# Gate columns moved beside v, four small VectorE steps per batch folded away, and the order of all steps written out

## The chip, the cores and the metric

The kernel runs on one core of one Trainium2 chip. TensorE (PE) multiplies matrices, VectorE (DVE) and ScalarE (ACT) do elementwise work, GpSimd (POOL) does elementwise work and indirect DMAs, and the SyncE queue (SP) issues the other DMAs. The metric is the time of one execution in device microseconds (us), as the median of several runs.

## What is computed

Linear attention feeds a mixture of experts that sends each token to one expert. There are 8 batches, 8 heads, 576 positions and a head width of 64; the experts take 4608 tokens of width 512, there are 8 of them, and their hidden width is 1024.

```python
q_s = exp(q - max(q, -1)); q_s /= sum(q_s, -1) + 1e-9
k_s = exp(k - max(k, 2));  k_s /= sum(k_s, 2) + 1e-9
x = einsum('bhsd,bhde->bhse', q_s, einsum('bhsd,bhse->bhde', k_s, v))   # rows of 512
logits = x @ w_gate; expert = argmax(logits); p = softmax(logits)[expert]
out = p * (relu(x @ w1[expert]) @ w2[expert])
```

## The kernel before

The program has two parts. The **attention stage** goes through the 8 batches. A batch is cut into steps, each a short Python function named by two or three letters, the batch and a number. A planner (`Plan.emit`) with a table of costs (`COST`), a table of due times (`WHEN`) and a list of fills (`FILL`) decides in which order the steps are written out; every engine then works through its own list in that order. The **expert stage** is a loop over tiles of up to 384 tokens of one expert, with the two matrix products in split precision (three products each, lines 983 and 999).

The steps of a batch b, with the lines at which the profile shows them:

- `LK`, `LV`, `LQ` load k, v and q (lines 206 to 223; on SP). q has one buffer, so `LQ` of a batch waits until the one before has been used up.
- `KM0` to `KM4` find the maximum of k (lines 340 to 358): `KM0` takes maxima of two tensors in SBUF on DVE (`kp`, `km`), `KM2` and `KM4` transpose on PE.
- `KS`, `KE`, `KR`, `ER` subtract it (DVE, line 374) and take exponentials (ACT, line 378).
- `KV` multiplies k by v (PE, line 392). A column of ones beside v gives the sums over k; `N0` adds two of its parts, `N1` adds 1e-9 (line 402) and takes the reciprocal, `N2` scales into the tile `kx` (ACT, line 410).
- `G0` to `G3` form `kx` times `w_gate` and put the result, 16 columns, at the end of each of the four blocks of `kx`, behind 128 columns of v and 2 of ones.
- `QM` takes maxima of q (DVE, line 457), `QS` subtracts on POOL (line 462), `QE` does a quarter of the work on ACT (line 476), and `QMR` and `QSR` do the remaining rows of two batches together.
- Per 128 tokens, `TR` transposes (PE), `EX` takes the exponential (ACT), `MM` multiplies by `kx` (PE, lines 515 and 518), `DE` and `RE` make the reciprocal of the denominators (DVE), and `EV` writes the result with two multiplies (DVE): line 530 the gate columns into `lh`, line 532 the 512 values into a row of `xr`.
- Routing of a batch (`LS`, `R0` to `RH`, lines 562 to 624, nearly all on DVE) sums the gate columns over the heads, finds the expert, and counts ranks with a product on PE (`R5`). `PU` (POOL, line 628) sends each row of 520 floats to its expert's place in the table `xs` in DRAM.

`WG`, `WH`, `WL` bring in w1 of expert 0, eight parts through three buffers; `IL` reads the first 384 rows back when batches 0 to 4 are sent; `L1` (line 720) and `L4` (line 734) are the expert products of that first tile, written out inside the attention stage. Step tables (`T0` to `T9`) follow. **Fills** (line 194) are products of ones that are never read, placed ahead of named steps on PE.

Two of the steps that the text below speaks of most:

```python
def n1():
    TS(ks, ks, EPS, None, op0=ALU.add)
    nc.vector.reciprocal(o.kr, ks)
```

Of the kernel before, what the change touches and what calls it, by code (L numbers as in the profile page):

```python
# [24 lines left out]
WARM, WARM0, WARMD = 40, 4.0, 0.6  # L25
HOT = 384
ON_ACT = (1, 1, 1, 1, 1, 1, 1, 1)
COST = dict(VG=1.5, VH=1.0, VL=1.2, LK=3.3, LV=4.0, LQ=3.3, CD=1.1, CS=1.31, KM0=2.2, KM1=0.7, KM2=0.45, KM3=0.6, KM4=0.95,
            KR=0.6, ER=0.58, KS=0.6, KE=0.58, VC=1.411, VR=0.52, KV=0.85, N0=0.1, N1=0.25, N2=0.67, G0=0.5, G1=0.56, G2=1.0,
            G3=0.18, QM=2.2, QE=0.48, QMR=0.6, QS=1.9, QSR=1.1, TR=0.48, EX=0.545, MM=1.05, DE=0.12, RE=0.16, EV=0.75, LS=0.6,  # L30
            R0=0.15, R1=0.17, R3=0.12, R4=0.12, R5=0.1, R6=0.13, R7=0.1, R8=0.15, R9=0.17, RA=0.1, RB=0.1, RC=0.11, RD=0.1,
            RE_=0.1, RF=0.1, RG=0.1, RH=0.14, PU=1.13, WM=0.22, WG=0.75, WH=0.54, WL=1.3, IC=0.062, ID=0.07, IL=2.25, IT=0.43,
            IH=0.57, IX=0.64, IM=0.1, IN=0.13, L1=2.08, L2=0.49, L3=0.55, L4=5.6, T0=0.049, T1=0.4, T2=0.2, T3=0.041, T4=0.13, T5=2.6,
            T6=0.33, T7=0.25, T8=0.6, T9=0.6, PD=7.0, SW=0.0)
WHEN = dict(VG=112.97, VH=65.802, VL=234.696, WM=178.215, LK=-4.311, LV=-2.99, LQ=-2.988, CS=-160.111, CD=-2.432, KM0=186.18,
            KM1=182.9, KM2=-234.498, KM3=140.412, KM4=-65.994, KR=-100.451, ER=-11.026, KS=48.242, KE=-18.137, VC=128.428,
            VR=170.02, KV=-48.753, N0=161.745, N1=-131.023, N2=90.74, G0=-78.547, G1=-207.944, G2=2.387, G3=-189.242, QM=-84.744,
            QE=-340.111, QMR=-76.618, QS=-126.151, QSR=-25.154, TR=47.844, EX=-122.752, MM=67.147, DE=-122.56, RE=-49.933,
            EV=23.487, LS=80.974, R0=-147.601, R1=102.567, R3=-18.581, R4=-14.182, R5=38.348, R6=-9.574, R7=-183.452,
            R8=-116.162, R9=-214.4, RA=-219.99, RB=-108.906, RC=-268.039, RD=-23.486, RE_=-237.132, RF=29.438, RG=-216.006,  # L40
            RH=126.679, PU=95.896, WG=2.331, WH=-51.233, WL=-94.387, IC=109.395, ID=319.612, IL=0.595, IT=-86.61, IH=55.938,
            IX=158.381, IM=-20.084, IN=-124.88, L1=172.533, L2=98.456, L3=63.079, L4=63.079, T0=-143.724, T1=85.977, T2=96.711, T3=-20.217,
            T4=135.561, T5=67.264, T6=-338.231, T7=192.024, T8=-120.773, T9=1000.0, PD=179.626, SW=73.996)
WINDOW = 0.0
FILL = """
KM2.0.0.24 KM4.0.0.1 KM2.1.0.18 KM4.1.0.4 KV.0.0.1 KV.0.1.1 KM2.2.0.13 G2.0.0.1 KV.1.1.1 KV.1.2.1 KM2.3.0.4 G0.1.0.7
KM4.3.0.1 TR.1.2.1 KV.2.2.1 R5.0.0.2 MM.1.4.4 KV.3.2.1 G0.3.0.9 TR.3.2.1 G2.3.0.2 KV.4.0.1 KV.4.1.1 KV.4.2.1 KM2.5.0.16
KV.4.3.2 R5.2.0.1 MM.3.0.1 MM.3.1.2 MM.3.2.2 MM.3.3.2 TR.3.4.2 G2.4.0.2 KV.5.2.1 G2.5.0.2 MM.5.0.4 MM.5.1.4 TR.5.4.1
KM4.7.0.14 KV.6.0.1 KV.6.1.1 KV.6.2.1 G0.6.0.5 TR.6.2.2 KV.7.2.1 IT.4.1.1 IT.4.2.4 MM.7.0.1 MM.7.4.2
# [5 lines left out]
class Plan:  # L55

    LAG = {SP: 1.8, PE: 0.2, DVE: 0.2, ACTE: 0.2, POOL: 0.2}
    ISSUE, PUT, PUT_LAG = 1.4, 0.75, 1.2  # L60

# [7 lines left out]
    def start(self, a, x):
        if a.key[0] == "PU":  # L70
            return a.done
        if a.eng == x.eng:
            return a.end - a.us if x.eng == SP else a.end + 0.1 if x.eng == DVE else a.end
        return a.end + self.LAG[a.eng]

    def emit(self, fill):
        fills = {(name, int(b), int(i)): int(n) for name, b, i, n in (w.split(".") for w in FILL.split())}
        todo = dict(self.steps)
        for x in todo.values():
            x.after = [self.steps[a] for a in x.after if a in self.steps]  # L80
            x.until = [self.steps[a] for a in x.until]
            x.end = None
        free = dict.fromkeys(self.LAG, 0.0)
        dma = 0.0
        taken = {t: [] for t in self.bufs}
        line = sorted((x for x in todo.values() if x.eng == SP), key=lambda x: x.rank)
        wait = list(todo.values())
        ready = []
        while wait or ready:
            rest = []  # L90
            for x in wait:
                (rest if any(a.end is None for a in x.after) else ready).append(x)
            wait = rest
            best = []
            for x in ready:
                if x.eng == SP and x is not line[0]:
                    continue
                t = max([free[x.eng], x.at] + [self.start(a, x) for a in x.after])
                if x.take and len(taken[x.take]) >= self.bufs[x.take]:
                    old = taken[x.take][-self.bufs[x.take]].until  # L100
                    if any(a.end is None for a in old):
                        continue
                    t = max([t] + [self.start(a, x) for a in old])
                best.append((t, x.rank, x))
            t0, _, first = min(best, key=lambda y: y[:2])
            t, _, x = min((y for y in best if y[2].eng == first.eng and y[0] <= t0 + WINDOW), key=lambda y: y[1])
            if x.eng == SP:
                line.pop(0)
                free[SP] = t
                dma = x.end = max(dma, t + self.ISSUE) + x.us  # L110
            else:
                free[x.eng] = x.end = t + x.us
            if x.key[0] == "PU":
                dma = max(dma, x.end + self.PUT_LAG) + self.PUT
                x.done = dma + self.LAG[SP]
            if x.take:
                taken[x.take].append(x)
            ready.remove(x)
            fill(fills.get(x.key, 0))
            x.fn()  # L120
# [3 lines left out]
def attention_moe(ctx: ExitStack, tc: tile.TileContext, q, k, v, w_gate, w1, w2, xs, out):  # L124
# [1172 lines left out]
```

## Time and profile before

| | us |
|---|---|
| median of 3 runs | 606.98 (606.12 to 607.13) |
| the profiled execution | 607.46 |
| its span, first to last instruction | 605.7 |
| attention stage, until `L1` starts on PE | 161.5 |
| PE / DVE / ACT / POOL busy in the span | 586.4 / 328.5 / 239.2 / 132.7 |

The span is 1.8 us shorter than the execution's own time. Busy shares over the whole span say little here: the attention stage and the expert stage have different limits, so the stages are read apart.

### The profile page before, as it was taken

The page shows a single profiled execution, that of the slowest core. Times are in us where ns is not written, and L with a number is a line of the kernel's source. Part 1 is how long each engine was busy: PE and PEld are TensorE (multiplying, and loading weights), DVE is VectorE, ACT ScalarE, POOL GpSimd, SP SyncE. Part 2 cuts the span into 40 slices and gives each one's busy share as a digit, 9 for nine tenths or more (in the row PEclk, how much of TensorE's full clock was granted, in tenths as well). Part 3 has the DMA queues.
Part 4 walks back from the last instruction along what each step waited for, and adds up shares of the span by engine and source line. Part 5 has one row for each costly group of instructions (what it writes and reads, how often), then busy time and mean ns, then how long its engine had stood idle before and what let it go on. Part 6 is the DMA issues. An engine that isn't in the chain of part 4 may idle for free.

```text
span 605.7 us, 11670 instructions
## 1 busy us (share of the span) xinstructions
PE 586.4 (97%) x3942; PEld 514.3 (85%) x3943; DVE 328.5 (54%) x686; ACT 239.2 (39%) x495; POOL 132.7 (22%) x210
## 2 busy tenths in 40 slices
PE   8899999999999999999999999999999999999996
PEld 4577867777897889989898989898989999898995
DVE  5779989998870242627041413245717552672566
ACT  1657537665521222524131222225516342542453
POOL 3122565676441001020101010011010201101020
PEclk9999999999999999999999999999999999999999
DMA  9999999894665821071703020304170634245000
GB/s 243 286 267 255 297 286 272 246 261 164 240 230 172 266 50 55 18 225 34 203 6 87 17 65 22 70 35 122 75 226 17 195 126 117 54 149 189 19 26 5
DMA packets 85309, 86.20 MB, mean 142 GB/s; under 512 B 21024, under 2 KB 70688, under 8 KB 84641
## 3 DMA queue, kind: packets, MB, share of 16 engines
q1 hardware_dynamic: 79280, 66.82, 40.7%
q0 software_dynamic: 6000, 19.03, 8.4%
q8 instruction: 16, 0.26, 0.2%
q14 instruction: 13, 0.10, 0.1%
HBM read 63.88 MB, written 22.74 MB: 143 GB/s over the span
## 4 chain that ended last, share of the span: by engine, by line
PE 83%; DVE 9%; ACT 2%; issue 2%; DMA 2%; SPq 1%; POOL 1%; POOLq 0%; DVEq 0%; ACTq 0%
PE py L999 32%; PE pt L983 25%; PE ph L983 8%; PE kv L392 3%; PE ph L720 3%; PE xp L515 2%; PE py L1025 2%; DMA kt<-in_k 2%; DVE qm L457 1%; PE hot L194 1%; DVE xr L532 1%; PE kg L194 1%; ACT kx L410 1%; PE qT L503 1%; PE py L734 1%
## 5 line engine op out<-in xcount | busy, mean ns | idle before, releaser
L999 PE MATMUL py<-w2h,hid 128*128 128x512 f32 x576 | 179.9, 389 | 0.0
L1131 DVE SCALAR_TENSOR_TENSOR hid<-pt,hid 128x384 fp32r<-128x384 f32 x84 | 46.3, 556 | 213.1 <-ACT hid L1066 212.9
L999 PEld LDWEIGHTS py<-w2h,hid 128*128 128x128 f32 x576 | 108.1, 188 | 22.2 <-issue 0.3
L1180 POOL DMA_INDIRECT out<-yt,ix x39 | 43.3, 1109 | 320.4 <-ACT yt L1057 320.4
L999 PE MATMUL py<-w2l,hid 128*128 128x512 f32 x288 | 112.1, 389 | 0.0
L1057 ACT ACTIVATE yt<-py,ga 128x512 f32<-128x512 f32 x39 | 26.8, 687 | 147.6 <-PE py L999 133.9
L1066 ACT ACTIVATE hid<-pt 128x384 fp32r<-128x384 f32 x84 | 41.2, 491 | 96.2 <-PE pt L983 87.7
L983 PE MATMUL pt<-xh,w1h 128*128 128x384 f32 (+1 forms) x336 | 64.5, 313 | 0.9 <-issue 0.9
L983 PE MATMUL pt<-xh,w1l 128*128 128x384 f32 (+1 forms) x336 | 64.4, 313 | 0.0
L983 PE MATMUL pt<-xl,w1h 128*128 128x384 f32 (+1 forms) x336 | 64.4, 313 | 0.0
L999 PEld LDWEIGHTS py<-w2l,hid 128*128 128x128 f32 x288 | 54.1, 188 | 10.7
L983 PEld LDWEIGHTS pt<-xh,w1h 128*128 128x128 f32 x336 | 54.5, 189 | 2.4 <-DVE xl L1124 1.3
L983 PEld LDWEIGHTS pt<-xl,w1h 128*128 128x128 f32 x336 | 54.0, 189 | 0.0
L983 PEld LDWEIGHTS pt<-xh,w1l 128*128 128x128 f32 x336 | 54.0, 189 | 0.0
L628 POOL DMA_INDIRECT xs<-xr,posi x36 | 37.3, 1037 | 42.1 <-DVE lh L530 20.0
L1119 DVE STREAM_TRANSPOSE xrow<-xt 128x1536 f32<-128x1536 f32 x14 | 41.2, 2941 | 3.7 <-DMA gx<-xs 3.7
L515 PE MATMUL xp<-kx,qTs 128*128 128x146 f32 x256 | 37.2, 291 | 1.6 <-ACT qTs L508 1.0
L515 PEld LDWEIGHTS xp<-kx,qTs 128*128 128x128 f32 x256 | 33.4, 190 | 3.9 <-DVE xr L532 1.8
L194 PEld LDWEIGHTS <-ones 128*128 128x128 bf16 x216 | 21.7, 102 | 14.3 <-issue 2.9
L462 POOL TENSOR_TENSOR qs<-qt,qm 128x1024 f32<-128x1024 f32 (+1 forms) x16 | 23.8, 1512 | 41.6 <-DVE qm L457 35.6
L508 ACT ACTIVATE qTs<-qT 128x512 f32<-128x512 f32 x36 | 21.1, 595 | 26.5 <-PE xp L515 15.3
L392 PE MATMUL kv<-vt,kt 128*64 128x65 f32 (+1 forms) x640 | 29.7, 230 | 0.6 <-DMA vt<-in_v 0.6
(207 smaller groups left out, 841.2 us busy)
## 6 DMA issues: line engine op xcount, KB each, us to landing
raw<-in_moe_w SPq DMA_DIRECT2D x10, 2048.0 KB, 9.0
vt<-in_v SPq DMA_DIRECT2D x16, 512.0 KB, 9.4
qt<-in_q SPq DMA_DIRECT2D x8, 1024.0 KB, 7.1
kt<-in_k SPq DMA_DIRECT2D x7, 1024.0 KB, 9.1
xt<-xs SPq DMA_DIRECT2D x32, 192.0 KB, 5.1
xs<-zr SPq DMA_DIRECT2D x11, 260.0 KB, 3.2
xt<-in_moe_w SPq DMA_DIRECT2D x8, 256.0 KB, 5.9
raw<-in_moe_w SPq DMA_DIRECT2D x4, 512.0 KB, 5.8
```

The source lines that it names most:

```text
L194: nc.tensor.matmul(hot.t, ones16, ones16[:, None, :].to_broadcast([P, HOT // P, P]), start=True, stop=True)
L392: nc.tensor.matmul(o.kv[i * D:(i + 1) * D, c, lo:lo + D + 1], o.kt[:r, 2 * c + i, j, :], VT[b % 2][:r, 2 * c + i, at:at + D + 1], start=Fa ...
L462: nc.gpsimd.tensor_tensor(o.qs[:, j0:j1].rearrange("p j h d -> p h j d"), o.qt[:, :, j0:j1, :], o.qm[:, :, j0:j1, None].to_broadcast([P, H ...
L515: nc.tensor.matmul(xv[:, c, :KW], o.qT[i][:, c, :], kx[:, c, :], start=True, stop=True)
L628: s = nc.gpsimd.indirect_dma_start(out=xs, out_offset=bass.IndirectOffsetOnAxis(ap=n.pi[:, t - t0:t - t0 + 1], axis=0), in_=xr[:, t, :], i ...
L983: m = e.matmul(ph, wt[:, c, f * P:(f + 1) * P], xt[:, c, :w], start=(n == 0), stop=(n == 3 * NC - 1))
L999: m = e.matmul(g.PY[u], ht[:, f, u * P:(u + 1) * P], wt[:, f, :], start=(n == 0), stop=(n == 3 * NF - 1))
L1057: m = e.activation(g.YT[u], g.PY[u], AF.Copy, scale=g.GA[:, u:u + 1]).wait_op(sPY[u], cu[u], GE)
L1066: e.activation(g.HH[:, f, :], g.PH[f][:, :W], AF.Relu).wait_op(sPH[f], it, GE).then_inc(sHH[f], 1)
L1119: e.transpose(g.XR.rearrange("p c (k j) -> p k c j", j=32), xblocks(g.XT).rearrange("p k (l c) -> p k c l", c=NC)).wait_op(sX, ld, GE).the ...
L1131: e.scalar_tensor_tensor(g.HL[:, f, :], g.PH[f][:, :W], 0.0, g.HH[:, f, :].bitcast(F32), op0=ALU.max, op1=ALU.subtract).wait_op(sHH[f], it ...
L1180: e.indirect_dma_start(out=g.out, out_offset=bass.IndirectOffsetOnAxis(ap=g.IX[:, u:u + 1], axis=0), in_=g.YT[u], in_offset=None, bounds_c ...
```

## The change

- **Gate columns.** A block of `kx` is now 8 gate columns, 128 of v, 8 gate columns, then 2 of ones: the same 146. The columns of one head and its gates lie together, so one multiply of 576 values writes all of it into a row of `xr` (`EV`, line 524 of the changed kernel). A row of `xs` has 584 floats. `LS` sums over heads and columns in `xr` itself, with longer strides; `lh` is gone. Loads from `xs` pick their 128 columns out of blocks of 144, and the first ones come as four pieces of 512 bytes per row and a separate load of the last 8 floats.
- **Folded steps.** The 1e-9 of `N1` enters through the product that clears the sums (`eps16`, in three parts). In routing, `R7` (running count) merges into `R6`, `RA` and `RF` (place of the expert's rows) into one more small product of `R5` with `place`, and `RE_` (adding 1e-9) into a column of `pb` that `RC` sums as well.
- **Order.** Planner, costs and due times are gone; one list, `ORDER`, gives every step and the number of fills ahead of it. There are 184 fills in place of 216 (40 warm ones and 176 of the list).
- **Expert stage.** `AHEAD`: PE does 4 parts instead of 3 of a product ahead of the transposes of the first tile.

```diff
-            nc.tensor.matmul(t, none16[:1].to_broadcast([1, P]), none16[:1, :, None].to_broadcast([1, NP, D + 2]), **flags)
+            nc.tensor.matmul(t, ones16[:65], eps16[:65], **flags)
...
         def n1():
-            TS(ks, ks, EPS, None, op0=ALU.add)
             nc.vector.reciprocal(o.kr, ks)
...
         def ev(i):
             xv, qd = o.xp[i], o.qd[i]
-            TT(o.lh[:, i].rearrange("p (c i) e -> p c i e", i=2), xv[:, :, 2 * D + 2:KW].rearrange("p c (i e) -> p c i e", i=2),
-               qd[:, :, :, None].to_broadcast([P, NP, 2, E]), op=ALU.mult)
-            TT(xr[:, i, :DM].rearrange("p (c i d) -> p c i d", c=NP, i=2), xv[:, :, :2 * D].rearrange("p c (i d) -> p c i d", i=2),
-               qd[:, :, :, None].to_broadcast([P, NP, 2, D]), op=ALU.mult)
+            TT(xr[:, i, :XW].rearrange("p (c i d) -> p c i d", c=NP, i=2), xv[:, :, :KG].rearrange("p c (i d) -> p c i d", i=2),
+               qd[:, :, :, None].to_broadcast([P, NP, 2, D + E]), op=ALU.mult)
...
         def lsum():
-            RED(lg, o.lh[:, sl].rearrange("p t h e -> p t e h"), op=ALU.add, axis=AX.X)
+            g = xr[:, sl, :XW].rearrange("p t (c x e) -> p t e c x", c=NP, e=E)[:, :, :, :, 0:KG // E:KG // E - 1]
+            RED(lg, g, op=ALU.add, axis=AX.XY)
...
-            nc.tensor.matmul(rk[:, :T], ones16, acc[prev][:, None, :].to_broadcast([P, T, E]), start=False, stop=(T == 1))
+            nc.tensor.matmul(rk[:, :T], ones16, place[:, None, :].to_broadcast([P, T, E]), start=False, stop=False)
+            nc.tensor.matmul(rk[:, :T], ones16, n.acc[:, None, :].to_broadcast([P, T, E]), start=False, stop=(T == 1))
...
-        add("RA", b, r, DVE, a8, [("R4", b, r)])
-        add("RE_", b, r, DVE, a12, [("RC", b, r)])
-        add("RF", b, r, DVE, a13, [("RD", b, r), ("RA", b, r)])
...
-    plan.emit(fill)
+    plan.emit(ORDER, fill)
```

**What moves on DVE.** The first place is DVE behind the maxima of q of batch 4 (`qm`). Before, the routing sum of batch 2 and then `kp` and `km` of batch 5 stand right behind it:

```order
L457 TENSOR_REDUCE qm<-qt 128x32
L562 TENSOR_REDUCE own<-lh 128x32
L340 TENSOR_TENSOR kp<-kt 128x512
L341 TENSOR_TENSOR km<-kp 128x256
L566 TENSOR_REDUCE lm<-own 128x4
L340 TENSOR_TENSOR kp<-kt 128x512
L341 TENSOR_TENSOR km<-kp 128x256
```

In the changed kernel, `kp` and `km` of batch 5 are long done at that place, and the subtraction of the maxima from k of batch 5 (`kt`) stands there:

```order
L454 TENSOR_REDUCE qm<-qt 128x32
L600 TENSOR_REDUCE posi<-rs 128x4
L603 RECIPROCAL xr_118<-own 128x4
L517 TENSOR_SCALAR qden<-xp 128x8
L375 TENSOR_TENSOR kt<-kt,mb 128x2x256
L375 TENSOR_TENSOR kt<-kt,mb 64x8x64
L375 TENSOR_TENSOR kt<-kt,mb 128x2x256
```

So `kp`, with two operands in SBUF, no longer follows the maxima there; `kt` has one operand, `mb`, in PSUM.

**What moves on SP.** The second place is the SP queue from the second load of q to the third, before:

```order
L220 DMA qt_385<-in_q 128x8x256
L212 DMA vt1_92<-in_v 128x8x128
L223 DMA qr_258<-in_q 64x8x64
L215 DMA vt1_92<-in_v 64x8x64
L206 DMA kt_472<-in_k 128x8x256
L208 DMA kt_472<-in_k 64x8x64
L212 DMA vt0_91<-in_v 128x8x128
L220 DMA qt_588<-in_q 128x8x256
```

And in the changed kernel:

```order
L215 DMA qt_555<-in_q 128x8x256
L207 DMA vt0_91<-in_v 128x8x128
L218 DMA qr_558<-in_q 64x8x64
L207 DMA vt0_91<-in_v 128x8x128
L218 DMA qr_558<-in_q 64x8x64
L201 DMA kt_562<-in_k 128x8x256
L210 DMA vt0_91<-in_v 64x8x64
L203 DMA kt_562<-in_k 64x8x64
L207 DMA vt1_92<-in_v 128x8x128
L648 DMA xt_84<-in_moe_w1 128x512
L215 DMA qt_752<-in_q 128x8x256
```

The rest of v of batch 1 is issued ahead of the second load of q, and all of v of batch 2, half of v of batch 3 and the first part of w1 now stand ahead of the third load of q.

**What moves on PE.** The third place is the end of the attention stage on PE. Before, the last product with `kx` (`xp`) is complete when the first product with w1 (`ph`) starts:

```order
L515 MATMUL xp<-kx_98,qTs 128x146 x8
L194 LDWEIGHTS ones_108
L194 MATMUL rk<-ones_108 128x384
L194 LDWEIGHTS ones_108
L194 MATMUL rk<-ones_108 128x384
L515 MATMUL xp<-kx_98,qTs 128x146 x4
L720 MATMUL ph_2374<-xh,w1h_61 128x384 x4
```

In the changed kernel, two `xp` and a transpose stand behind that first product:

```order
L509 MATMUL xp<-kx_98,qTs 128x146 x4
L700 MATMUL ph_2178<-xh,w1h_61 128x384 x4
L700 MATMUL ph_2178<-xl,w1h_61 128x384 x4
L700 MATMUL ph_2178<-xh,w1l_62 128x384 x4
L497 MATMUL qT<-ident,qs 128x128 x4
L509 MATMUL xp<-kx_98,qTs 128x146 x4
```

One step of w1 work now lies between the last products with `kx`, and there are no fills at this place.

## Rows read from the trace of the kernel before

**Rows 1.** Windows: us, busy of PE, PEld, DVE, ACT, POOL, clock, DMA, GB/s
```profile
40.00:146.00 106.00, 101.04 (x1126) 81.38 (x1121) 98.57 (x288) 64.49 (x179) 56.74 (x77) 1.00 0.95 261
146.00:161.50 15.50, 14.72 (x125) 12.83 (x122) 12.14 (x50) 8.57 (x21) 8.39 (x17) 1.00 0.71 252
...
200.00:606.00 406.00, 399.80 (x2208) 365.44 (x2208) 172.35 (x214) 138.97 (x236) 44.45 (x51) 1.00 0.30 90
```

**Rows 2.** Chain that ended last, end of the attention stage: start, us, what
```profile
160.77 0.60 DVE xr L532
161.37 0.10 DVE pe L570
161.47 0.04 issue
161.51 2.34 PE ph L720 x12
...
194.35 1.44 PE pt L1041 x12
```

**Rows 3.** Waits of DVE, 40 to 146 us: total us, times, longest
```profile
DVE rs L605 <- PE rk L194: 1.6, 1, 1.6
DVE own L399 <- PE kv L392: 1.1, 1, 1.1
```

**Rows 4.** Fills: weight loads of line 194, and a run of 16 in the timeline
```profile
L194 PEld LDWEIGHTS <-ones 128*128 128x128 bf16 x216 | 21.7, 102 | 14.3 <-issue 2.9 <-DVE none L257 1.8
...
84.90 2.77 PE L194 MATMUL kg<-ones 128*128 128x384 bf16 x16
87.51 0.60 PE L349 MATMUL kmT<-ident,km 128*128 128x128 f32 x4
```

**Rows 5.** Timeline of DVE: start, us, line, operation (starts give the spacing)
```profile
93.23 0.17 DVE L402 TENSOR_SCALAR own<-own 128x4 f32<-128x4 f32 x1
93.43 0.18 DVE L403 RECIPROCAL kr<-own 128x4 f32<-128x4 f32 x1
...
155.01 0.16 DVE L601 TENSOR_SCALAR cm<-own 128x4 f32<-128x4 f32 x1
155.13 0.17 DVE L614 TENSOR_SCALAR own<-own 128x4 f32<-128x4 f32 x1
155.21 0.16 DVE L523 TENSOR_SCALAR qden<-xp 128x8 f32<-128x8 f32 x1
...
159.10 0.22 DVE L530 TENSOR_TENSOR lh<-xp,qden 128x64 f32<-128x64 f32 x1
159.24 0.68 DVE L532 TENSOR_TENSOR xr<-xp,qden 128x512 f32<-128x512 f32 x1
159.84 0.15 DVE L523 TENSOR_SCALAR qden<-xp 128x8 f32<-128x8 f32 x1
```

**Rows 6.** Groups of DVE reductions by form: busy us, mean ns of one
```profile
L457 DVE TENSOR_REDUCE qm<-qt 128x32 f32<-128x2048 f32 x8 | 18.2, 2276 | 2.0 <-DMA qt<-in_q 2.0
...
L562 DVE TENSOR_REDUCE own<-lh 128x32 f32<-128x256 f32 x4 | 2.4, 601 | 0.0
```

**Rows 7.** Timelines of DVE and of POOL at 81 and at 115 us
```profile
80.95 0.68 DVE L340 TENSOR_TENSOR kp<-kt 128x512 f32<-128x512 f32 x1
81.67 0.42 DVE L341 TENSOR_TENSOR km<-kp 128x256 f32<-128x256 f32 x1
82.13 3.86 DVE L340 TENSOR_TENSOR kp<-kt 128x512 f32<-128x512 f32 x1
...
115.50 2.93 DVE L341 TENSOR_TENSOR km<-kp 128x256 f32<-128x256 f32 x1
...
82.48 2.94 POOL L462 TENSOR_TENSOR qs<-qt,qm 128x1024 f32<-128x1024 f32 x2
...
115.64 2.49 POOL L677 TENSOR_TENSOR w1l<-xt,w1h 128x512 fp32r<-128x512 f32 x2
```

**Rows 8.** Timeline of DVE at the third q; GB/s of 40 slices of the page
```profile
47.19 2.29 DVE L457 TENSOR_REDUCE qm<-qt 128x32 f32<-128x2048 f32 x1
...
GB/s 243 286 267 255 297 286 272 246 261 164 240 230 172 266 50 55 18 225 34 203 6 87 17 65 22 70 35 122 75 226 17 195 126 117 54 149 189 19 26 5
```

**Rows 9.** The tile qt: users (ns min/median/max, first and last start), landing of loads
```profile
L476 ACT ACTIVATE qs<-qt,qm x64: 331/333/349, 20.4 to 142.3; 128x64 f32<-128x64 f32 x64
...
L457 DVE TENSOR_REDUCE qm<-qt x8: 2268/2274/2286, 18.1 to 136.7; 128x32 f32<-128x2048 f32 x8
...
DMA to landing us min/median/max: 6.1/7.1/11.1
```

More of the change, by code (lines that the diff above doesn't have):

```diff
@@ L18, with thirds @@
 EPS = 1e-9
-WSTEP = 0.15
+def thirds(x):
+    parts = []
+    for _ in range(3):
+        parts.append(struct.unpack("<f", struct.pack("<I", struct.unpack("<I", struct.pack("<f", x))[0] & 0xFFFF0000))[0])
+        x = struct.unpack("<f", struct.pack("<f", x))[0] - parts[-1]
+    return parts
 CUT = 5
-AHEAD = 3
+AHEAD = 4
 W2POOL = 0
@@ L35 @@
[L35 to L43, printed above, removed]
@@ L69, in start @@
[L69 to L84, printed above, removed]
-        taken = {t: [] for t in self.bufs}
[L86 to L115, printed above, removed]
@@ new lines, in add, with emit @@
+    def add(self, name, b, i, eng, fn, after=(), take=None, until=()):
+        self.steps[name, b, i] = SimpleNamespace(eng=eng, fn=fn, after=list(after), take=take, until=list(until))
+    def emit(self, order, fill):
+        words = [w.split(".") for w in order.split()]
+        queue = [(name, int(b), int(i)) for name, b, i, *_ in words]
+        assert sorted(queue) == sorted(self.steps)
+        seen = set()
+        taken = {t: [] for t in self.bufs}
+        for key, word in zip(queue, words):
+            x = self.steps[key]
+            assert all(a in seen for a in x.after if a in self.steps), key
@@ L116, in emit @@
             if x.take:
+                if len(taken[x.take]) >= self.bufs[x.take]:
+                    assert all(a in seen for a in taken[x.take][-self.bufs[x.take]].until), key
                 taken[x.take].append(x)
-            ready.remove(x)
-            fill(fills.get(x.key, 0))
+            seen.add(key)
+            fill(int(word[3]) if len(word) > 3 else 0)
             x.fn()
@@ L269, in attention_moe @@
     spacer = cst.tile([1, 1], F32, name="spacer")
-    acc = {(-1, 0): cst.tile([P, E], BF, name="acc0", tag="acc", bufs=3)}
+    OH = [cst.tile([P, SLOT + 1, E], BF, name=f"oh{i}") for i in range(B + 2)]
+    place = cst.tile([P, E], BF, name="place")
+    PB = [cst.tile([P, SLOT, E + 1], F32, name=f"pb{i}") for i in range(2)]
+    turn = {(-1, 0): 0}
     done = {}
@@ L360, in kmax @@
         for i in range(parts):
-            add("KM0", b, i, DVE, lambda i=i: f0(i), [("LK", b, 0 if b else i), ("KM0", b, i - 1)], part=1 / parts, take=None if i else "km", until=[("KM2", b, 0)])
+            add("KM0", b, i, DVE, lambda i=i: f0(i), [("LK", b, 0 if b else i), ("KM0", b, i - 1)], take=None if i else "km", until=[("KM2", b, 0)])
         add("KM1", b, 0, DVE, f1, [("LK", b, 1 if b else 2), ("KM0", b, parts - 1)])
@@ L543, in xtiles @@
             add("RE", b, t, DVE, lambda t=t: rec(t), [("DE", b, t)])
[L544 removed]
+            add("EV", b, t, DVE, lambda t=t: ev(t), [("RE", b, t), ("PU", b - 2, t)])
     written = []
@@ L889, in attention_moe @@
     tables()
-    for n in range(WARM):
-        add("WM", 0, n, PE, lambda: fill(1), at=WARM0 + n * WARMD, take=None if n else "xp", until=[("WM", 0, WARM - 1)])
-    plan.emit(fill)
+    plan.emit(ORDER, fill)
     nc.gpsimd.memset(spacer, 0.0)
```

255 lines of the change are left out of this document (141 added, 114 removed).

## The prediction, made before the changed kernel ran

> **What bounds the kernel now.** I cut the span into windows by stage first, because one share over 606 us would mix two kernels. From 200 us on, PE is busy 399.8 of 406 us: the expert stage is PE's own work, which the change leaves alone, so what the stages before it gain or lose arrives at the end one for one [rows 1]. The chain of waits shows where the attention stage is handed over: a DVE write of a row of `xr` ends, and 0.14 us later the first product with w1 starts, at 161.51 [rows 2]. From there PE runs on into the transposes of the first expert tile at 194.35 without a wait, so one more part of a product ahead of them (`AHEAD`) has nothing to hide and is costed at nothing; if the rows were late there it would hide up to a part's length.
>
> Inside the attention stage, from 40 to 146 us, PE is busy 101.0 of 106 and DVE 98.6 of 106 [rows 1]. The two are not alike. PE's time holds 216 fills over the whole stage, and 16 of them in a row take 2.6 us (84.90 to 87.51), 0.163 us each, 35 us in all [rows 4]: much of PE's busy time is waiting that has been filled. DVE's work is all needed, and its longest wait in that stretch is 1.6 us, the next 1.1 [rows 3]. So DVE sets the pace there; in the last 15 us it has slack (12.1 of 15.5 busy) and PE and the hand-over set the end.
>
> A third resource is near its limit: in the first three slices of the page, 45 us, the DMA queues move 243, 286 and 267 GB/s, 265 on average, and stay above 245 until 136 us [rows 8]. Loads of q are the ones used soonest after they land.
>
> **The change part by part.** Durations are taken from start to next start, since DVE instructions overlap in the records.
>
> *EV as one multiply.* The gate multiply `lh` takes 0.14 us (159.10 to 159.24) and the multiply of 512 values 0.60 [rows 5]. One multiply of 576 values I take in proportion, 0.60 × 576/512 = 0.675, so a tile saves 0.065; if the width cost nothing it would be 0.14, and if the longer one cost as much as both, 0. In 40 to 146 us there are 28 tiles (5 of batches 1, 3 and 5, 4 of batches 2 and 4, 3 of batch 0 and 2 of batch 6): 1.8 us, between 0 and 3.9.
>
> *N1.* The addition of 1e-9 takes 0.20 us (93.23 to 93.43) [rows 5]. Seven batches have theirs on DVE in the saturated stretch: 1.4 us. The product that clears the sums reads 65 rows where it read one; it has the same columns and stands where fills stand, so it is costed at nothing.
>
> *Four routing steps.* `RA` takes 0.12 (155.01 to 155.13) and `RE_` 0.08 (155.13 to 155.21) [rows 5]; `RF` and the running count `R7` are as small, and I take 0.08 each: 0.36 per batch, six batches, 2.2 us. The added product with `place` is one of 8 columns per tile on PE, among fills.
>
> *LS.* The sum still adds 256 values for 4 tiles, at 0.601 us in a group that takes over twice the time per value of the contiguous maxima (2.276 us for 2048) [rows 6]. Strides grow from 32 to over 500 bytes. I take no change. Bounds: 256 values at the contiguous pace, 0.28, saves 0.3 a batch, 1.9 us over six; twice as slow costs 0.6, 3.6 us.
>
> *Moves on DVE.* At 82.13 `kp` takes 3.86 us where its twin at 80.95 took 0.68; in the same time, 82.48 to 85.4, POOL runs the subtraction `qs`. At 115.50 `km` takes 2.93 instead of 0.42 while POOL splits w1, 115.64 to 118.1 [rows 7]. That is 3.2 and 2.5 us of DVE busy with nothing. The changed order puts `kt` behind the maxima at the first place, and I count its 3.2 us as gained. Where `km` meets the split of w1 in the new order can't be read without times, so its 2.5 are not counted. Bounds 0 and 5.7. By the Trainium skill (SBUF — State Buffer, Who interferes with whom) an instruction of VectorE with two SBUF inputs and one of GpSimd that reads SBUF lock each other out for the whole instruction, and one that reads PSUM for one input does not; the trace agrees with 3.86 against 0.68 us, and by that rule alone the first would be saved in full.
>
> *Moves on SP.* Ahead of the third load of q now stand two parts of v of 0.52 MB, one of 0.13 and a part of w1 of 0.26: 1.44 MB more, at 265 GB/s 5.4 us [rows 8]. Before, the maxima of that q start at 47.19 [rows 8]; behind them in DVE's list stand the routing of batch 0 and the rows of batch 1. Of the 5.4 us DVE fills some 1.9 with work that is now listed ahead (two `EV`, a routing sum, 0.60 each, and small steps); 3.5 us it would stand still. Bounds 0 (the load is not late, because the queue has room) and 5.4.
>
> *Rows of 584 floats.* By 136 us some 18 tiles of rows are sent, each 33 kB longer, 0.6 MB, 2.2 us of DMA time at 265 GB/s. The queue has a slice at 164 GB/s right after, and I let this hide there; uncovered it costs 2.2.
>
> *End of the stage.* On PE a product with w1 (2.34 us) now stands ahead of the last two products with `kx` [rows 2], and so covers DVE's last writes. PE is idle 0.8 us in 146 to 161.5 [rows 1]; I count 0.7 as gained, between 0 and 2.3 (idle and fills there).
>
> *Sum.* Removed 1.8 + 1.4 + 2.2 = 5.4, the freed `kp` 3.2, the end 0.7, less the late q 3.5: 5.8 us less. The profiled execution took 607.46 for a span of 605.7, so it would be 601.7; against the median of 606.98 shown, 0.5 lower, **601.2**. A second count from PE's side: 32 fills fewer are 32 × 0.163 = 5.2 us less in its list, and nine more products of a few columns add little; with the same idle time PE ends 5 us sooner. Neither count uses the other's rows.
>
> **The rivals.**
>
> *More comes free.* Both lock-outs go and q is not late: 5.4 + 5.7 + 0.7 = 11.8. PE then stops it: 5.2 of fills and the idle of 40 to 161.5, 5.0 + 0.8, allow 11 at most. About 10, so 597. For it: nothing but `kp` and `km` of this kind stalls in [rows 7], and both moved. Against it: eight splits of w1 remain on POOL and must stand beside something.
>
> *The change does not shorten the path.* The instructions go but the loads set the pace: 5.4 + 0.7 gained, 5.4 lost to the late q, nothing of `kp`: 606.3. For it: 265 GB/s over 45 us. Against it: the queue falls to 246 and 164 GB/s later, so it catches up [rows 8].
>
> *Slower: the loop of q.* q has one buffer, so a load waits for the last use of the one before. A turn is maxima 2.27, subtraction 2.0 (of the 2.94 for its two parts, the first being twice as large), eight exponentials of 0.33, landing 7.1 (11.1 at worst): 14 to 18 us [rows 7, 9]. Before, the eight maxima run from 18.1 to 136.7, 16.9 us a turn [rows 9]. In the new list the exponentials of q stand behind some of k and behind a copy that waits for PE. If that adds two waits of 0.9 a turn becomes 18.7, and the last maxima start at 19.7 + 7 × 18.7 = 151. Behind them stand about 17 us until the first product with w1 (7.5 to the last subtraction, ten for PE's steps), 168 instead of 161.5: 613. It decides from 17.8 us a turn, where 19.7 + 125 + 17 reaches 161.5. My own sum has 16.9 to 17.
>
> **How the numbers follow.** The forecast has 0.60, more free 0.16, no shortening 0.10, the loop of q 0.14. A measurement of this kernel tells about 0.2% from no change, 1.2 us. The forecast's own range is 598 to 604.5; beyond it come the bounds: both lock-outs gone down to 596, a slow `LS` (3.6) or no freed `kp` (3.2) up to 605, the loads to 606.3. Range **596 to 606.5**, which leaves out the loop of q and a little below. Faster by over 0.2% is forecast and more free, with 0.02 of the forecast's own upper end given to the same: 0.74; same 0.12; slower 0.14.
>
> **What would show it.** In the changed profile: `L1` on PE starts at 155 to 156; DVE's multiply into `xr` is 36 instructions of about 0.75 us in the records (0.68 × 576/512), no `lh`, no `own` of line 402; `LS` stays near 0.6; no `kp` of 3.86 beside `qs`. The third maxima of q start at 50 to 52 with a DMA as releaser. The expert stage is the same 400 us of PE. I am wrong if DVE is not the engine that waits least in 40 to 146, if `kp` or `km` meets POOL elsewhere for as long, if DVE waits for q in every batch (the loop), or if a wait stands between the first expert tile's load and its transposes.

## The result: 1% slower, and the profile after

The changed kernel takes 613.08 us (median of 11 runs, 609.28 to 616.87) against 606.98 (606.12 to 608.85) for the kernel before, a ratio of 1.0095 [1.0074, 1.0115]. The prediction was 601.2 and faster. Run again later beside other kernels, where the kernel before itself took 614.70, the ratio was 1.0026 [1.0004, 1.0049]. The kernel before took 606.8 to 607.0 in this set of runs and in the last two (the branch moved with the pair of runs that compares the folded work, and the last two kernels of the experiments), and 613.6 to 614.7 in the three sets between; the later five sets each ran on another chip. So everything below is compared by its ratio to the runs of before beside it. Ratios from the two kinds of sets are not alike: the changed kernel's own is 1.0095 in one and 1.0026 in the other.

The profiled execution took 616.71 for a span of 614.9, 9.2 more than before. First the windows of [rows 1] again, then the end of the chain of waits (start, us, what).

```profile
40.00:146.00 106.00, 94.06 (x1006) 75.95 (x1004) 83.48 (x212) 60.35 (x169) 53.93 (x72) 0.95 0.94 263
146.00:161.50 15.50, 14.78 (x140) 13.20 (x139) 12.76 (x41) 9.61 (x28) 9.54 (x16) 1.00 0.40 114
200.00:606.00 406.00, 402.37 (x2221) 368.23 (x2220) 171.32 (x212) 140.48 (x237) 43.39 (x50) 1.00 0.31 94
```

```profile
160.98 2.27 PE ph L700 x12
163.26 0.44 PE qT L497 x4
163.69 1.00 PE xp L509 x8
...
164.82 1.10 PE xp L509 x8
...
184.79 3.64 DMA xs<-xr,posi
...
189.63 0.59 PE ph L1009 x2
190.22 9.81 PE py L1002 x36
200.03 1.44 PE pt L1018 x12
201.49 1.47 ACT xh L1039
202.98 1.77 DVE xl L1145
204.75 3.11 issue
207.86 7.22 PE pt L960 x32
```

DVE is busy 83.5 of 106 us where it was 98.6, and over the whole span 319.3 where it was 328.5: the work went, and idle time took its place. The first product with w1 starts at 160.98, as before (161.51), but two parts of `xp` stand behind it. Then the chain leaves PE: the last rows are sent to `xs` at 184.79 and land 3.6 us later, the barrier passes, and at 204.75, 4.7 us after the first transpose of the first expert tile, "issue" (the engine waits for nothing that the profile shows) stands for 3.11 us. The same end of the chain before, past the rows of [rows 2]:

```profile
185.41 0.83 issue
186.24 0.59 PE ph L1032 x2
...
195.79 3.44 PE py L1025 x15
199.23 0.88 issue
```

Reading the same points off both chains splits the 9.2:

| us, profiled execution | before | after | later by |
|---|---|---|---|
| last product of the attention stage ends | 185.4 | 187.5 | 2.1 |
| barrier passed, first product behind it | 186.24 | 189.63 | 1.3 more |
| first transpose of the first expert tile | 194.35 | 200.03 | 2.3 more |
| first product of layer 1 in the loop | 200.11 | 207.86 | 2.1 more |
| from there to the end of the span | 405.6 | 407.0 | 1.4 more |

So 7.1 of the 9.2 are lost from the barrier on, where I had costed the change at nothing. Of the 2.3 ahead of the transposes, 0.7 is the part that `AHEAD` moved there (36 products where 33 stood); with the branch moved, below, those 36 take 1.6 less, at full clock. Two kinds of rows show how. The windows (columns as in [rows 1]; the granted clock is the third last) show four stretches at half clock, 1.2 GHz, each behind a stop of PE; before had none up to 600 us.

```profile
85.70:88.10 2.40, 0.00 (x1) 0.00 (x0) 0.71 (x3) 0.89 (x2) 0.00 (x0) 1.00 0.92 276
88.10:94.90 6.80, 6.69 (x54) 5.44 (x55) 4.99 (x16) 0.23 (x1) 0.00 (x0) 0.50 1.15 302
125.70:129.10 3.40, 3.40 (x25) 2.63 (x26) 1.25 (x7) 1.26 (x4) 0.00 (x0) 0.50 0.93 267
190.50:193.90 3.40, 3.40 (x9) 2.63 (x8) 0.00 (x0) 0.49 (x1) 1.00 (x1) 0.50 0.70 157
207.60:211.00 3.40, 3.14 (x10) 3.17 (x11) 0.00 (x0) 0.00 (x0) 0.00 (x0) 0.50 1.05 369
```

The stops ahead of the first two wait for loads (DVE for k of batch 5 at 87.39, so PE behind it; PE for v of batch 6), the third for the barrier, the fourth for "issue". In the timeline, releasers in brackets:

```profile
87.39 0.68 DVE L345 TENSOR_TENSOR km<-km,kt 64x512 f32<-64x512 f32 x1 [2.62 <-DMA kt<-in_k]
122.97 0.45 PE L393 MATMUL kv<-vt,kt 128*64 128x65 f32 x8 [0.84 <-DMA vt<-in_v]
172.66 1.19 POOL L611 DMA_INDIRECT xs<-xr,posi  x1 [11.79 <-DVE xr L603]
189.63 0.59 PE L1009 MATMUL ph<-ones 128*128 128x512 bf16 x2 [2.17 <-SPq L883]
207.86 0.66 PE L960 MATMUL pt<-xh,w1h 128*128 128x384 f32 x1 [3.63 <-issue]
```

The third row is why the sends end late: POOL stands 11.8 us until DVE has routed batch 6. What the last row waits for is found at the line of the branch at the head of the expert loop, `e.If(kind < 5)`: count, ns minimum/median/maximum of its instruction on PE's sequencer, first and last start, before and then after (there with the maxima of q, by their line).

```profile
L1007 PEldq COMPARE_BRANCH  x14: 81/222/3650, 196.2 to 580.8; - x14
```
```profile
L984 PEldq COMPARE_BRANCH  x14: 71/212/6045, 201.5 to 590.0; - x14
L454 DVE TENSOR_REDUCE qm<-qt x8: 2273/2286/2287, 20.3 to 147.9; 128x32 f32<-128x2048 f32 x8
```

The longest is the first of its 14 passes. Before, it took 3.65 us from 196.2 on, under 15 products that were still queued and covered all but 0.88; now 6.05 from 201.5 on, under 12.

### The profile page after: what moved, and what is told of

Read it like the earlier page. It is cut to its first block, busy times and chain, and to the rows that moved or that the text cites. A ratio compares the mean times of both kernels' runs of the same rounds, so it can differ in the third digit from the quotient of the medians.

```text
span 614.9 us, 11592 instructions
## 1 busy us (share of the span) xinstructions
PE 588.0 (96%) x3919; PEld 517.8 (84%) x3920; DVE 319.3 (52%) x609; ACT 236.6 (38%) x495; POOL 132.6 (22%) x213
## 4 chain that ended last, share of the span: by engine, by line
PE 84%; DMA 5%; ACT 3%; DVE 3%; issue 2%; SPq 2%; POOL 1%; POOLq 0%; DVEq 0%; ACTq 0%
PE py L976 32%; PE pt L960 25%; PE ph L960 8%; PE kv L393 3%; PE xp L509 3%; PE hot L188 3%; PE ph L700 2%; DMA kt<-in_k 2%; PE qT L497 2%; DMA vt<-in_v 2%; PE py L1002 2%; DMA qr<-in_q 1%; SPq L648 1%; PE kg L188 1%; PE xp L512 1%
## 5 line engine op out<-in xcount | busy, mean ns | idle before, releaser
L509 PE MATMUL xp<-kx,qTs 128*128 128x146 f32 x256 | 39.1, 298 | 0.4 <-DVE xr L524 0.4
L393 PEld LDWEIGHTS kv<-vt,kt 128*64 128x64 f32 (+1 forms) x640 | 25.0, 141 | 11.9 <-issue 5.5
L393 PE MATMUL kv<-vt,kt 128*64 128x65 f32 (+1 forms) x640 | 31.5, 237 | 3.0 <-DMA vt<-in_v 1.4
```

The lines of the kernel that those rows point to most:

```text
L393: nc.tensor.matmul(o.kv[i * D:(i + 1) * D, c, lo:lo + D + 1], o.kt[:r, 2 * c + i, j, :], VT[b % 2][:r, 2 * c + i, at:at + D + 1], start=Fa ...
L509: nc.tensor.matmul(xv[:, c, :KW], o.qT[i][:, c, :], kx[:, c, :], start=True, stop=True)
```

## Experiments

Ratios are to the kernel before, with 95% intervals; all are within 2% of 1, and a kernel is called faster or slower here when its interval leaves out 1. Profiles are of one execution each. "The branch" is that of the rows above.

**Undo the order, or parts of it.** The folded work in the old order:

```diff
-AHEAD = 4
+AHEAD = 3
-ORDER = "LK.0.0 LK.0.1 LK.0.2 LK.1.0 LV.0.0 LK.1.1 ..."
+ORDER = "LK.0.0 LK.0.1 LK.0.2 LK.1.0 LK.1.1 LV.0.0 LQ.0.0 ..."
```

> All folded work of the change (wide multiply, no addition in N1, no RA, RE_, RF, R7), but steps and 216 fills in the order of before, and 3 parts ahead of the first tile. Theory A, the folding shortens DVE's path and the listed order loses it again: 606.98 less the 5.4 of the first term, 600.5 to 603.5, and the granted clock stays at 1 through the attention stage. Rival B, the folding is off the path or its longer rows and strides cost as much as it saves: 606 to 608. Rival C, the split loads of the first expert tile cost by themselves: 603.5 to 606, with more than 13.9 us from the barrier to the first part of layer 1.

0.9916 [0.9888, 0.9943]: theory A by the ratio. But the profiled execution (612.75, the longest of seven) has half clock at 139 and 156, and the branch takes 0.37. Of rival C the sign is there: from the barrier to layer 1 it is 14.0 us, 0.89 of them a wait for the split loads of the rows (`xt`). So the ratio mixes causes. The run that moves only the branch, and the pair with and without the folded work, take them apart (below).

> The changed kernel with five loads moved up in SP's queue: both loads of k of batch 5 behind the third of v of batch 4, and the three of v of batch 6 ahead of q of batch 5. Theory A, these late loads are what stops DVE and PE at 85 to 88 and at 122 to 124 us, and the half clock that follows comes from those stops: waits of 2.5 and 1.4 us go, and of 6.8 and 3.4 us at half clock up to half each, 3.4 and 1.7: 604 to 610, and no fall of the granted clock at 88 and 126. Rival B, the turn of the one q buffer (18.2 us) sets the pace, so the stall moves to q: 612 to 614.

```diff
-LV.4.1 ... LQ.2.1 LQ.3.0 LV.4.2 LQ.3.1 LK.5.0 WG.0.2 LK.6.0 LK.6.1 LK.5.1 ... LQ.5.0 LQ.5.1 WG.0.5 LV.6.0 LV.6.1 LV.6.2
+LV.4.1 LK.5.0 LK.5.1 ... LQ.2.1 LQ.3.0 LV.4.2 LQ.3.1 WG.0.2 LK.6.0 LK.6.1 ... LV.6.0 LV.6.1 LV.6.2 LQ.5.0 LQ.5.1 WG.0.5
```

1.0095 [1.0052, 1.0137], no better than the changed kernel: PE falls to half clock at 80.6 and 118.1 instead. Moving the two late loads only moved the stops: the first now comes behind a load of q that lands at 75.66, as rival B had it. So the place of these two loads in SP's queue is not by itself what makes PE stop.

> The changed kernel with fills where PE stood idle: 15 more ahead of the transposes of k of batch 5 (2.5 us), 9 more ahead of the first products of v of batch 6 (1.4 us) and 13 behind the last product of the attention stage (2.1 us). The late loads and sends stay late. Theory A, the half clock costs time of its own: 3.4 + 1.7 + 1.7 us at most come back, 606 to 611, and the granted clock stays at 1 at 88, 126 and 190. Rival B, the fall of the clock costs nothing, since PE has slack behind each wait: 612 to 614 with the clock at 1.

```diff
-KM2.5.0.2 ... KV.6.0.1
+KM2.5.0.17 ... KV.6.0.10
     plan.emit(ORDER, fill)
+    fill(13)
```

0.9991 [0.9963, 1.002], full clock up to 606 us. It looked like theory A, but the first product with w1 still starts at 160.69, so in the attention stage the fills cost about what the half clock had (160.98). The gain came at the branch, 0.37 us, which no theory had foreseen.

> The changed kernel, where the loads of the second expert's weights (4 MB) wait until DVE has written the low part of the first tile (about 205 us), instead of starting at 197. Theory A, PE's branch at the head of the expert loop, 6.05 us long, waits for code whose fetch stands behind these weights: the branch falls under 3.5 us, PE's idle time before the first part of layer 1 from 3.1 to under 1, the time by 2 to 4: 609 to 611. Rival B, the fetch is slow by itself or starts late: the branch stays at 5 to 6 us and the time at 612 to 614. Rival C, the second expert's weights now come too late: over 614, with PE waiting for them after 225 us.

```diff
+        e.wait_ge(sXL, 1)
         with e.If(x.get(LIVE, 1, 0, 1) > 0):
             wload(x.get(EO, 1, 0, E - 1), False)
```

1.0073 [1.0041, 1.0105], 619.35 us. The branch takes 3.47 us instead of 6.05, as theory A had it; but the loads of the next tile now stand behind the weights, and PE stands 4.5 us, until 228.68, behind one of them (`gx`, landed at 225.30): rival C by its time, though it isn't the weights that come late.

> The changed kernel with the fills of the run before it at two of the three places (15 more ahead of the transposes of k of batch 5, 9 more ahead of the products of v of batch 6, 5 at the end), and with the routing of batches 6 and 7 listed earlier on DVE and POOL, so that the rows of batch 6 are sent behind the last multiply instead of 12 us later. Theory A, the last sends hold the barrier: they end near 178 instead of 184.8 us, the barrier passes when PE is done, 187 to 188 instead of 189.6, and the time is 2 to 3 below that of the fills alone: a ratio to before of 0.993 to 0.997. Rival B, the barrier is not what the first expert tile waits for (its load is), so the ratio stays at 0.998 to 1.001.

```diff
-... RG.6.0 ... RH.7.0 RH.6.0 PU.6.0 IN.4.0 RH.7.3 PU.7.1 PU.6.3 ...
+... EV.7.4 RB.6.0 R9.6.0 RC.6.0 RD.6.0 RG.6.0 RH.6.0 PU.6.0 PU.6.1 PU.6.2 PU.6.3 R5.7.0 ...
     plan.emit(ORDER, fill)
+    fill(5)
```

0.995 [0.9928, 0.9973], the last send at 179.8 instead of 184.8; PE now sets the barrier (188.99, passed at 189.91), but waited 1.39 us for the routing moved ahead.

> The folded work in the order of before, with 4 parts ahead of the first tile as in the changed kernel, and 15 more fills at the two places where PE waited 1.2 and 1.5 us for ACT and its clock then fell (139 and 156 us). Theory A, these two stretches at half clock cost 1.7 us each: 2 to 3.5 below the old order without them, a ratio to before of 0.986 to 0.989. Rival B, they come only in the slower executions, so the median gains under 1: 0.990 to 0.992.

```diff
-G2.6.0 ... G2.7.0
+G2.6.0.7 ... G2.7.0.9
```

0.9926 [0.9898, 0.9955], full clock to 605, with 16 fills by its list: nearest to rival B; fills and half clock cost about the same again.

> The changed kernel as it is, beside the others on one chip. If its loss against before is its own, the ratio is again 1.007 to 1.012; if it came from that one chip, it is nearer to 1.

1.0026 [1.0004, 1.0049], nearer to 1. It took 616.44, no less than in the first set; the kernel before is what lost more:

> The kernel before as it is, for a profile beside the others on one chip. If its 614 us in the second set of runs (607 in the first) come from waits for loads and the half clock behind them, its granted clock falls in the attention stage there as well; if the chip is slower in all, the expert stage from 212 us on takes longer too.

One execution of 613.09; its expert stage is as long as ever, but PE falls to half clock in it too, and the first product with w1 starts at 167.56 instead of 161.51:

```profile
153.50:160.30 6.80, 6.47 (x32) 4.87 (x31) 3.14 (x9) 2.62 (x6) 0.00 (x0) 0.50 0.36 134
```

So the kernel before stands close to the same fall. In this pair the attention stage of the changed kernel ends 6.9 us sooner (184.5 against 191.4), and what follows loses 8.7, more than that (spans of 613.1 and 611.3).

**The branch.** Eight kernels now showed it short or long. One more moved the code behind it:

> The changed kernel with 60 products on PE that are never reached for the first tile (a branch for tiles of kind 0, in the body of the expert loop between the branch at its head and the code of the full-width layer 1). Everything that runs before stays; only the place of that code in PE's program moves, from instruction 1,744 to 1,806 as the program lists them. It was 1,744 or 1,778 in the kernels whose branch took 3.2 to 7 us, and 1,796 to 1,828 in those where it took 0.4. Theory A, the branch waits for code to be fetched and the place decides it: under 0.5 us instead of 6.05, 5.0 us from the end of the transposes to layer 1 minus their 1.6, no half clock behind it, so 4 to 5.5 us off: a ratio to before of 0.993 to 0.997 where the changed kernel had 1.0026. Rival B, the fills or the clock made those branches short, not the place: the branch stays at 6 and the ratio at 1.000 to 1.005.

```diff
             with e.If(kind < 5):
+                with e.If(kind < 1):
+                    for _ in range(60):
+                        e.matmul(g.PH[3], g.ones16, ...)
                 with e.If(kind < 4):
```

1.0144 [1.009, 1.0198], above both ranges, the branch 6.67 us: my theory of the code's place fell. Then the branch itself was moved:

> The changed kernel with 42 products of one column behind the last product of the attention stage, where PE waits 2.2 us for the barrier; they shift all later code of PE by 84 instructions, the branch at the head of the expert loop too, which the run before left in place. Theory A, the place of the branch itself decides: as the program lists PE's instructions, with weight loads counted, it stood at 2,479 to 2,525 in the kernels where it took 3.2 to 7 us and at 2,543 to 2,575 where it took 0.4, and here it is at 2,575. The branch falls from 6.05 to under 0.5 us, layer 1 starts 5.0 instead of 8.0 us after the first transpose, no half clock follows, and the time is 4 to 5.5 lower: a ratio of 0.993 to 0.997. Rival B, the place is chance and the fills made the difference: the branch stays at 6, the ratio at 1.000 to 1.015.

```diff
     plan.emit(ORDER, fill)
+    for _ in range(42):
+        nc.tensor.matmul(hot.t[:, :1], ones16, ones16[:, :1], start=True, stop=True)
```

0.9978 [0.9958, 0.9999], just above theory A's range, in a set where the kernel before takes 606.78. The branch and the maxima of q by their lines, and the hand-over in the chain of waits:

```profile
L986 PEldq COMPARE_BRANCH  x14: 81/222/462, 193.2 to 577.3; - x14
L454 DVE TENSOR_REDUCE qm<-qt x8: 2274/2276/2286, 19.7 to 141.0; 128x32 f32<-128x2048 f32 x8
```
```profile
182.96 0.59 PE ph L1011 x2
183.56 8.21 PE py L1004 x36
191.77 1.44 PE pt L1020 x12
193.24 1.46 ACT xh L1041
194.72 1.77 DVE xl L1147
196.49 0.04 issue
196.53 6.51 PE pt L962 x36
```

From the transposes to layer 1 it is 4.8 us instead of 7.8, "issue" 0.04 instead of 3.11. With every weight load counted, the branch stands at 2,479 to 2,525 in PE's program where it takes 3.2 to 7 us (nine profiles of seven kernels) and at 2,543 to 2,613 where it takes at most 0.46 (nine kernels). A jump over the same code is short or long by where the program put it. The traces show why: they hold DMA packets of the kind "instruction", and on queue 8 some 16 of 16 KB each. Which engine a packet is for is not recorded; its time beside the branch is what ties it to PE.

| kernel | the branch, us | packet of code nearest to it, us |
|---|---|---|
| before | 196.16 to 199.81 | 197.24 to 198.40 |
| changed | 201.51 to 207.56 | 205.16 to 206.05 |
| changed, weights later | 201.45 to 204.92 | 202.40 to 203.42 |
| changed, branch moved | 193.20 to 193.66 | 189.18 to 190.14 |

In each of the nine profiles with a long branch a packet starts 0.9 to 4.4 us into the branch, and the branch ends 2.3 to 2.6 us after that start; in the nine with a short one the packet has landed 2.7 to 3.6 us before the branch begins. By the Trainium skill (Runtime: NRT & Kernel Launch, Instruction fetch mechanics) a taken branch whose target is not in the code at hand waits until it is fetched by DMA; the trace agrees, with these packets and with 0.46 against 6.05 us for a shift of 84 instructions. Why the packet starts 1.1 us into the branch before and 3.65 us into that of the changed kernel stays open: with the weights later it is 0.95, but before loads the same weights beside its branch.

**What the folded work is worth.** The old order, with fewer fills:

> The folded work in the order of before, 4 parts ahead of the first tile, with 32 fills fewer (184, as many as in the changed kernel): the single ones and a third of three of the long groups. The code of layer 1 is kept in place by 70 products that are never reached. Theory A, in the old order PE with its fills is as long as DVE, so that DVE's 6 us less of work gave only 1.3 us at the last maxima of q; with 32 fills less, 5.2 us, the first product with w1 starts 3 to 5 us sooner, at 157 to 160, a ratio to before of 0.983 to 0.988. Rival B, what binds is the chain over PE, ACT and DVE with its latencies, not PE's own time: the fills were waits already, the first product with w1 stays at 161 to 163, and the clock may fall where PE now stands: 0.990 to 0.998.

```diff
-KV.0.0.1 KV.0.1.1 G0.1.0.7 G0.3.0.9 KM4.7.0.14 ...
+KV.0.0 KV.0.1 G0.1.0.5 G0.3.0.6 KM4.7.0.9 ...
```

0.9966 [0.9929, 1.0004], within rival B's range. The last maxima of q come at 133.0, but half clock at 137 and 151 loses it (first product with w1 at 164.82), and the branch, at 2,479, takes 5.77. Then 22 of these fills were taken out, and 9 put in at two other places, with and without the folded work:

> The folded work in the order of before, 4 parts ahead, with 22 fills fewer up to the transposes of k of batch 7 (the single ones, 2 and 3 of two groups), and 9 more at the two waits before products with the gates in batches 6 and 7; 20 products of one column at the start keep the branch of the expert loop where it was short (2,556). Theory A, PE with its fills is what DVE's folded work was hidden behind: the last maxima of q at 133 to 134 instead of 135.4, the first product with w1 at 158 to 161, no half clock: a ratio of 0.983 to 0.988. Rival B, what is gained before 133 us is lost again in the last part, where PE, ACT and DVE wait for each other: the first product with w1 at 162 to 163, 0.990 to 0.994.

> The kernel before, nothing folded, with the same fills taken out and put in. Theory A, DVE's work sets its pace, as the prediction said: without the fills PE waits for DVE instead, the last maxima of q stay at 136 to 137.5, and the ratio is 0.997 to 1.004; the folded work alone then makes the difference to the run beside it. Rival B, the fills themselves were the length: the last maxima of q come 2 to 3 us sooner here too, and the ratio is 0.990 to 0.996.

```diff
-KV.0.0.1 KV.0.1.1 ... G0.1.0.7 ... G0.3.0.9 ... G2.6.0 ... G2.7.0
+KV.0.0 KV.0.1 ... G0.1.0.5 ... G0.3.0.6 ... G2.6.0.4 ... G2.7.0.5
```

0.9959 [0.9934, 0.9984] with, 1.0075 [1.0043, 1.0107] without. Maxima of q (first and last start), with and then without:

```profile
L454 DVE TENSOR_REDUCE qm<-qt x8: 2269/2276/2287, 18.1 to 133.6; 128x32 f32<-128x2048 f32 x8
```
```profile
L456 DVE TENSOR_REDUCE qm<-qt x8: 2268/2277/2287, 18.3 to 135.6; 128x32 f32<-128x2048 f32 x8
L1006 PEldq COMPARE_BRANCH  x14: 71/212/6505, 196.2 to 586.1; - x14
```

The first products with w1 start at 159.08 and 161.37. Without the folded work, 13 fills fewer on balance gain 0.1 us there against [rows 2]: PE's fills did not set the pace, which fits DVE. The profile with the folded work has half clock at 19.3 and 80.7, 3.4 us each, the other none before the products with w1, so the 2.3 us between them may be low. The loss of 1.0075 is the branch, which slid to 2,498 with the fills and takes 6.50 where it took 3.65, with 6.8 us of half clock behind it.

**The changed kernel, mended.**

> The changed kernel with fills at three waits of PE (15 ahead of the transposes of k of batch 5, 9 ahead of the products of v of batch 6, 10 ahead of the third last product with kx) and the rows of batches 6 and 7 sent sooner, the sums of batch 6 left where they were on DVE so that PE doesn't wait 1.4 us for them as it did in the first try; none at the end. Theory A, hand-over and clock were what the changed order lost: PE's last product of the attention stage ends near 186.5, the barrier at 187.4, layer 1 at 201: a ratio to before of 0.989 to 0.993. Rival B, the stage itself is held by the turn of q and gains nothing from it: 0.994 to 0.997.

```diff
-KM2.5.0.2 ... KV.6.0.1 ... MM.7.2
+KM2.5.0.17 ... KV.6.0.10 ... MM.7.2.10
```

0.9956 [0.9933, 0.998], with the sends placed nearly as in the run of 0.995; full clock to 607, but the first product with w1 at 162.18 (rival B).

> The changed kernel with the branch of the expert loop moved (42 products of one column and 5 fills fewer, now at the start) and the rows of batches 6 and 7 sent sooner. Theory A, hand-over and place of the branch were all that the changed kernel lost, and its attention stage is shorter as predicted: the barrier 0.9 us behind PE's last product instead of 1.4 to 2.2, layer 1 near 195 to 198, a ratio to before of 0.992 to 0.997 where moving the branch alone gave 0.998. Rival B, the last sends were no wait once PE is done: 0.997 to 0.999. Rival C, sending sooner puts routing ahead of work that PE waits for: over 0.999.

```diff
-KM2.0.0.33
+KM2.0.0.28
+... EV.7.4 R9.6.0 RC.6.0 RD.6.0 RG.6.0 RH.6.0 PU.6.0 PU.6.1 PU.6.2 PU.6.3 R5.7.0 ...
+    for _ in range(42):
+        nc.tensor.matmul(hot.t[:, :1], ones16, ones16[:, :1], start=True, stop=True)
     plan.emit(ORDER, fill)
```

0.9966 [0.9946, 0.9985]: the barrier stands 0.91 us behind PE's last product, layer 1 in the loop starts at 196.38, and the kernel is faster than both that were compared, by 0.3% against before. The 42 small products stand ahead of the attention stage here, not behind it.

> The same with 15 and 9 more fills where PE waits for k of batch 5 and v of batch 6. Theory A, they keep the clock up in the executions in which these loads come late and cost little in the others: the median 0 to 2 below that of the run beside it, and a narrower spread. Rival B, where the loads come in time they only lengthen PE's list, 24 fills of 0.16 us: 1 to 4 above it.

```diff
-KM2.5.0.2 ... KV.6.0.1
+KM2.5.0.17 ... KV.6.0.10
```

1.0072 [1.0047, 1.0097]: rival B and more. The first product with w1 starts at 158.33 instead of 155.38, and the longer program has a stop of its own inside layer 1, with a packet of code from 200.14 to 201.08 in it and half clock behind it. From layer 1 to the end it takes 410.0 us instead of 405.7, more than the fills cost ahead of it:

```profile
199.33 0.62 PE L962 MATMUL pt<-xh,w1h 128*128 128x384 f32 x2 [0.56 <-DVE xl L1147]
202.39 0.62 PE L962 MATMUL pt<-xh,w1h 128*128 128x384 f32 x2 [2.43 <-issue]
```

## Why the prediction was wrong

**The step that failed** is the first one: "From there PE runs on into the transposes of the first expert tile at 194.35 without a wait, so one more part of a product ahead of them (`AHEAD`) has nothing to hide and is costed at nothing", and that "what the stages before it gain or lose arrives at the end one for one". The hand-over was not free in the kernel before: it held a branch of 3.65 us, which 15 queued products covered but for 0.88, and that 0.88 of "issue" stood in its chain. The changed kernel left 12 (the part that `AHEAD` moved ahead is three products), its branch stands 34 instructions nearer to the start of PE's program, and it took 6.05. Shown: moving the branch, by small products behind the attention stage or at its start, brings the transposes-to-layer-1 time from 7.8 to 4.8 us, and the rest of the span from 407.0 to 405.7. The part moved ahead had something to hide as well: with three parts and the split loads PE waits 0.89 us for the rows. With branch and last sends mended the kernel takes 605.40 where before takes 606.97. That is 7.7 of the 11.9 us between forecast and result (601.2 and 613.08); the other 4.2 I put to an attention stage that gains less than I had summed. That I named "a wait between the first expert tile's load and its transposes" as what would make me wrong came near the place: the long wait stands behind the transposes, and it is for code.

**The end of the stage**, counted as 0.7 gained, cost 1.3 at the barrier: I followed PE's list there and not POOL's, on which the rows of batch 6 went out at 172.66 instead of 157.9. The run that sends them sooner, besides moving the branch, agrees: the wait at the barrier is 0.91 us, as before.

**Removed DVE work, 5.4 us.** Its parts were sized right: the multiply takes 0.753 us (0.75 predicted), `LS` 0.616 (0.6), and DVE is busy 9.2 us less over the span (which holds the shorter `kp` too). In groups by form:

```profile
L524 DVE TENSOR_TENSOR xr<-xp,qden 128x576 f32<-128x576 f32 x36 | 27.1, 753 | 0.6
...
L556 DVE TENSOR_REDUCE own<-xr 128x32 f32<-128x256 f32 x4 | 2.5, 616 | 0.1
```

On the path less of it was found: 2.3 us (159.08 against 161.37) in the same order with the same fills, in one pair of profiles, the shorter with 6.8 us of half clock. That DVE set the pace fits these runs; that all of the removed time would arrive does not. DVE's two longest waits in 40 to 146 us are then for PE, 2.5 and 2.2 us, where the longest without the folded work is 1.5. I take PE with ACT between its steps to come next; no run tells it apart from the half clock.

**`kp` and `km`.** No `kp` takes 3.86 any more. The longest is 1.75:

```profile
L341 DVE TENSOR_TENSOR kp<-kt x16: 639/684/1753, 4.6 to 124.7; 128x512 f32<-128x512 f32 x16
```

**The late third q.** Its maxima start at 53.36 with the load as releaser, said for 50 to 52. The wait itself is 0.90 us. What came late behind it were k of batch 5 and v of batch 6, which the term did not hold.

**The stage as a whole** came near the sum only where PE did not stop. I had the first product with w1 at 155 to 156, but two parts of `xp` and a transpose, 2.5 us, now stand behind it, so its start does not measure the same thing in both kernels. The last product of the stage, at 185.4 before, ends at 180.6 in the best execution (the branch moved), 4.8 us sooner where I had 5.8, at 181.9 in the mended kernel, and at 184.5 and 187.5 in the two of the changed kernel itself. In the six executions of its order of the attention stage without added fills the first product with w1 starts at 154.03 (no half clock ahead of it in the profile), 155.38, 157.97 and 159.35 (one whole stretch of 3.4 us each), 160.98 (10.2 us in two) and 161.16 (6.8 us). By how much the half clock itself delays it, and by how much the stops ahead of it, stays open: fills that kept the clock up cost as much (160.69; 158.33 against 155.38). Why the loads come late in some executions is open too.

**The rivals.** The loop of q was given 613 us, which is the time measured, but not for its reason. A turn was 18.2 us ((147.9 − 20.3)/7), over the 17.8 from which it was to decide; yet the first product with w1 was no later than before, because 13 us and not 17 lie between the last maxima and it. DVE waited for a load of q four times in eight, 4.0 us in all, so not in every batch. In the kernel with the branch moved, a turn in the same order was 17.3 us ((141.0 − 19.7)/7). The second count, PE's 32 fills at 5.2 us, said nothing of what fills are for: in the changed kernel PE's first long stop is ahead of the transposes of k of batch 5, where 16 of them had stood [rows 4] and 2 are left.

## What to carry to other kernels

Read the hand-over between two stages as a stage: what PE's sequencer does there (a branch, a barrier, a loop's first pass) is covered only as far as products are queued in front of it, and an edit elsewhere, even taking out fills, can move a branch to where it must wait for its code. The packets of code in the trace show whether it does. Before an instruction list is shortened, ask which engine is next, and by how little: here, of 5.4 us removed, one pair of profiles shows 2.3. And compare profiles in which the clock stayed up, or count the half-clock stretches first; executions of one order differ here by up to 7 us at the end of one stage, more than the whole gain forecast.

## What had not been expected of the hardware

- One branch takes 0.37 to 0.46 us or 3.2 to 7.0, long up to instruction 2,525 and short from 2,543 on in programs of some 3,300, and long just where a 16 KB packet of code starts inside it.
- Half clock came behind short stops: a granted clock of 0.50 for 6.8 us behind 2.4 us without products (85.70 to 88.10), and for 3.4 us behind the 2.17 us at the barrier.
